# Padding the tiles of v to 128 rows, and moving weight-conversion passes and batch loads later

## The chip, the cores and the metric

The kernel runs on one core of a Trainium2 chip. The metric is the device time of one execution in microseconds (us). Engines are named as in the profile: PE (TensorE matmul), PEld (its weight loads), DVE (VectorE), ACT (ScalarE), POOL (GpSimd) and SP (SyncE, which issues nearly all DMAs here). L578 means line 578 of the kernel.

## The reference, cut to what matters

```python
# attention: 4 batches, 8 heads, 576 positions, head size 64
mask_plain = (rel >= 0) & (rel < 32)                       # heads 0..3
mask_dil   = (rel >= 0) & (rel < 128) & (rel % 4 == 0)     # heads 4..7
attn = softmax(where(mask, q @ k.T / 8, -1e9))
x = (attn @ v) laid out as (2304 tokens, 512)
x = ((x @ w_a) * (x @ w_b)) @ w_out                        # 512 -> 1536 -> 512
# top-1 of 8 experts by cosine similarity; gate = softmax probability of the chosen one
out[mask_e] = gate * (relu(x @ w1[e]) @ w2[e])             # 512 -> 1024 -> 512
```

The weights `w_a`, `w_b` and `w_out` come in as 64-bit floats, every other array as 32-bit floats.

## The kernel before, in words

**Attention in tiles of 64 queries.** The host reorders the dilated heads so that both masks become a band: a tile of 64 queries meets 96 keys. A batch has 9 tiles. q and k come in groups of three tiles (`qkt`, 128 rows, 832 KB), v in groups of three tiles (`vt`, 96 rows of keys by 3 tiles by 512 columns, 576 KB). A tile goes through scores (PE), row maxima (`amx`, DVE) and their scaled copy (`least`, POOL), `exp` (four activations on ACT), `norm` (two small DVE operations, then a POOL multiply, L559), `trans` (PE transposes into one PSUM bank `tp`, then an ACT copy to `aT`), `av` (PE, L474 or L578) and `oevac` (ACT and DVE write x0 as a high and a low part).

**Every large product is three matmuls.** A 32-bit operand is split into a high part (ACT, L660) and the remainder (DVE or POOL, L661); `mm3` (L702 to L704) multiplies high by high, high by low and low by high.

**Order of the work.** The schedule is manual: each engine runs its instructions in program order. Batch 0's attention stands by itself at the start (loop at L1185, up to about 33 us), with its loads, the load of the first weights and a few warm-up matmuls between. Then come, for each batch b, twelve steps `f_step(b, f)` (x @ w_a, x @ w_b for 128 of the 1536 columns, their product g) and `x1_run` (times `w_out`). In the steps of batch b the attention of batch b+1 runs beside, as five pairs of tiles (the last pair has one tile). For b = 0 a pair takes an odd and an even `f`: pair p opens in step 2p+1 (called here the opening step: maxima, exp(0), norm(0)) and goes on in step 2p+2 (the closing step: exp(1), norm(1), trans(0)); trans(1) and av come at the start of the next opening step. In the code's own words the opening step has `odd` = 0, since b = 0 counts with a lag of one.

**One step of batch 0 on PE.** `mm(0,0)`, then in an opening step av of the pair before and the scores of this one, `mm(1,0)`, in a closing step trans(0), then `mm(0,1)`, `mm(1,1)`. Each `mm` is 12 matmuls into one of four PSUM banks; ACT's `a_copy` and DVE's `g_evac` (L745) empty them, ACT makes gh (L748) and POOL makes gl (L749) from g.

**The conversion.** Step n of batch 0 also converts the 64-bit weights of step n+2 (`conv_steps`, L627): a scale pass on ACT (L640), then on DVE a shift pass (L642), a sign pass (L644) and a low-word pass (L646), each over 128x1024 words. The next step's `ab_split` splits what the step before converted, so its high half on ACT waits for the low-word pass. `conv(cg, k)` issues the next k of the four passes. A load of 1 MB (`conv_load`) and a store of the converted 512 KB (`conv_store`) go with each.

**Before the change** the passes stand: in a closing step the scale pass ahead of exp(1), the shift pass ahead of norm(1), the sign pass after norm(1), the low-word pass at the end; in an opening step the scale and shift passes ahead of `ab_split`, the sign pass after `oevac` (ahead of exp(0) in the program, though on another engine), the low-word pass at the end.

**Buffers.** The pool `ld` has two buffers each for `qkt` and `vt`; a third load waits for the tile that used the buffer. The pool `ab` has two tiles for the split weights.

Of the kernel before, what the change touches and what calls it, by code (L numbers as in the profile page):

```python
# [8 lines left out]
F32 = mybir.dt.float32  # L9
# [8 lines left out]
B, H, S, D = 4, 8, 576, 64  # L18
# [63 lines left out]
def fused_kernel(ctx: ExitStack, tc: tile.TileContext, qk, v, wab, wout, w1, w2, emb, tau, cst, msk, out, dbg=None):  # L82
# [279 lines left out]
    ap = ab_ctx.enter_context(tc.tile_pool(name="ab", bufs=2, side="right"))  # L362
# [10 lines left out]
    qkt, vt = {}, {}  # L373

    ld_seq = [(b, g) for b in range(B) for g in range(3)]
    ld_pos = [0, 0]
# [8 lines left out]
    def load_v():  # L385
        if ld_pos[1] < len(ld_seq):
            b, g = ld_seq[ld_pos[1]]
            ld_pos[1] += 1
            vt[b, g] = ld.tile([96, 3, 512], F32, tag="v", name="vt")
            nc.sync.dma_start(out=vt[b, g], in_=v[b, g])  # L390

    x0 = {}
# [4 lines left out]
    class Attn:  # L397
# [69 lines left out]
        def av(self):  # L467
            b, j = self.b, self.j
            t, jj = vt[b, j // 3], j % 3
            self.o = ps.tile([128, 4, 64], F32, tag="mm2" if self.early and j % 2 else "av", name="av")  # L470
            for pr in range(4):
                for p in range(2):
                    h = 2 * pr + p
                    nc.tensor.matmul(  # L474
                        out=self.o[64 * p:64 * p + 64, pr, :],
                        lhsT=t[:, jj, 64 * h:64 * h + 64],
                        rhs=self.aT[:, pr, 64 * (p ^ pr % 2):64 * (p ^ pr % 2) + 64],
                        start=True, stop=True,
                    )
# [14 lines left out]
    class AttnPair:  # L494
# [76 lines left out]
        def av(self):  # L571
            self.o = ps.tile([128, 4, 64 * self.n], F32, tag="av", name="av")
            for i, j in enumerate(self.js):
                t, jj = vt[self.b, j // 3], j % 3
                for pr in range(4):
                    for p in range(2):
                        h = 2 * pr + p
                        nc.tensor.matmul(  # L578
                            out=self.o[64 * p:64 * p + 64, pr, 64 * i:64 * i + 64],
                            lhsT=t[:, jj, 64 * h:64 * h + 64],  # L580
                            rhs=self.aT[i][:, pr, 64 * (p ^ pr % 2):64 * (p ^ pr % 2) + 64],
                            start=True, stop=True,
                        )
# [23 lines left out]
    def conv_load(i):  # L607
        if i < len(conv_src):
            if i < NF and i % 3 == 2:
                c64[i] = mp.tile([128, 2048], I32, tag="wo", name="c64w", bufs=1)  # L610
            elif i in (NF + 2, NF + 3):
                c64[i] = ap.tile([128, 2048], I32, tag="ab", name="c64a")
            else:
                c64[i] = cv.tile([128, 2048], I32, tag="c64", name="c64")
            nc.sync.dma_start(out=c64[i], in_=conv_src[i].bitcast(I32))
# [34 lines left out]
    def conv(gen, n=4):  # L650
        for _ in range(n):
            next(gen, None)

    def ab_load(n):
        if NF <= n < n_ab:
            ab_raw[n] = raw_tile("abr")
            nc.sync.dma_start(out=ab_raw[n], in_=wab32[n % NF])
# [65 lines left out]
    def f_step(b, f, pairs, extra, extra2):  # L723
        n = b * NF + f
        acc = acc_pre if n == 0 else {}
        lag = 1 if b == 0 else 0
        p, odd = divmod(f - lag, 2)
        cur = pairs[p] if 0 <= p < len(pairs) else None
        prv = pairs[p - 1] if not odd and 0 <= p - 1 < len(pairs) else None

        def mm(c, hf):
            for k in range(2 if (c, hf) in acc else 0, 4):
                ab_mm(n, acc, c, hf, k)

        kept = {}

        def a_copy(hf):
            kept[hf] = ap.tile([128, HALF], F32, tag="a", name="a")
            nc.scalar.activation(out=kept[hf], in_=acc[0, hf], func=AF.Copy)

        def g_evac(hf):
            g = ap.tile([128, HALF], F32, tag="g", name="g")
            c = hf * HALF + CARRY * (1 - b % 2)
            t = slice(c, c + HALF)
            nc.vector.tensor_tensor(out=g, in0=kept[hf], in1=acc[1, hf], op=ALU.mult)  # L745

            def low():
                nc.scalar.activation(out=g_hl[0][:, f, t], in_=g, func=AF.Copy)  # L748
                nc.gpsimd.tensor_tensor(out=g_hl[1][:, f, t], in0=g, in1=g_hl[0][:, f, t].bitcast(F32), op=ALU.subtract)  # L749

            g_low.append(low)

        if f - lag in (3, 6, 9):
            load_qk()
        if f - lag in (5, 8, 11):
            load_v()
        if f < NF - 2:
            ab_load(n + 2)
        if b == 0 and n < 10:
            conv_load(n + 4)  # L760
        if n == NF - 1:
            conv_load(NF + 2)
        if b == 0:
            conv_store()
        cg = iter(())
        if b == 0:
            cg = conv_steps(n + 2)
        if cur is not None and odd:
            conv(cg, 1)
            cur.exp(1)  # L770
            conv(cg, 1)
            cur.norm(1)
            conv(cg, 1)
        if prv is not None:
            prv.trans(1)
        if not odd or cur is None:
            conv(cg, 2)
        if n == 0:
            for q in range(4):
                ab_split_part(1, q)  # L780
        elif f < NF - 1:
            ab_split(n + 1)
        elif b == 0:
            wo_split(0)
        mm(0, 0)
        a_copy(0)
        if not odd:
            if cur is not None:
                cur.open()
            if prv is not None:  # L790
                prv.av()
            if cur is not None:
                cur.scores()
                cur.least_of()
            if prv is not None:
                prv.oevac()
            conv(cg, 1)
        g_lows()
        mm(1, 0)
        if cur is not None and not odd:  # L800
            cur.exp(0)
        g_evac(0)
        if cur is not None and odd:
            cur.trans(0)
        g_lows()
        for x in extra:
            x()
        mm(0, 1)
        a_copy(1)
        for x in extra2:  # L810
            x()
        mm(1, 1)
        if cur is not None and not odd:
            cur.norm(0)
        g_evac(1)
        del ab_hl[n]
        conv(cg)
# [347 lines left out]
    with tc.manual_schedule():  # L1165
# [17 lines left out]

        early_conv = conv_all()
        for i in range(NJ + LAG + 1):  # L1185
            if i in (3, 6, 9):
                load_qk()
            if i in (4, 6, 9):
                load_v()
            if i == CONV1:  # L1190
                conv_load(1)
                nc.sync.dma_start(out=c_sb, in_=cst)
            if i == 6:
                conv_load(2)
            if i < NJ:
                gr[i].scores(early=True)
            if 1 <= i < NJ + 1:
                gr[i - 1].exp()
            if LAG <= i < NJ + LAG:
                gr[i - LAG].trans()  # L1200
                gr[i - LAG].tevac()
            if LAG + 1 <= i:
                gr[i - LAG - 1].av()
            keep_warm(N_WARM if i < 4 else N_WARM_LATE if i < WARM_TO else 0, "mm1" if (i + 1 - LAG) % 2 else "tp")
            if 1 <= i < NJ + 1:
                gr[i - 1].norm()
            if i == NJ + LAG:
                conv(early_conv, CONV_STEPS[i])
            if LAG + 1 <= i:
                gr[i - LAG - 1].oevac()  # L1210
            if i < NJ + LAG:
                conv(early_conv, CONV_STEPS[i])
            for q in range(4):
                if SPLIT0[q] == i:
                    ab_split_part(0, q)
            if i in PRE:
                for k in range(2):
                    ab_mm(0, acc_pre, PRE.index(i), 0, k)
        for _ in early_conv:
            pass  # L1220
        load_v()

        router = None
# [197 lines left out]
def layout(inputs):  # L1421
# [13 lines left out]
    kT = np.zeros((B, 128, 4, S + 32), np.float32)  # L1435
    kT[..., 32:] = kp.reshape(B, 4, 2, S, D).transpose(0, 2, 4, 1, 3).reshape(B, 128, 4, S)
    qk = np.zeros((B, 3, 128, 4, 416), np.float32)
    vb = np.zeros((B, 3, 96, 3, 512), np.float32)
    vz = np.zeros((B, S + 32, 512), np.float32)
    vz[:, 32:] = vp.transpose(0, 2, 1, 3).reshape(B, S, 512)  # L1440
    for g in range(3):
        qk[:, g, :, :, :192] = qT[..., 192 * g:192 * g + 192]
        qk[:, g, :, :, 192:] = kT[..., 192 * g:192 * g + 224]
        for i in range(3):
            j = 3 * g + i
            vb[:, g, :, i] = vz[:, 64 * j:64 * j + 96]
    wab = np.stack([bits['moe_w_a'], bits['moe_w_b']], 0).reshape(2, 4, 128, NF, 128).transpose(3, 2, 1, 0, 4).reshape(NF, 128, 1024)
    wo = bits['moe_w_out'].reshape(NPAIR, 2, 128, DM).transpose(0, 2, 1, 3).reshape(NPAIR, 128, 1024)

# [54 lines left out]
```

## Time and profile before

| | |
|---|---|
| median of 3 runs | 792.83 us (792.18, 792.83, 796.73) |
| the profiled execution | 793.86 us, of which the span of the trace is 792.0 us |
| PE busy | 774.6 us, 98% |
| DVE, ACT, POOL busy | 518.8, 410.1, 206.2 us |
| granted TensorE clock, mean | 0.995 |
| moved by DMA | 136.18 MB, 172 GB/s over the span |

The profile has the busy time of each engine, slices of the span, the chain of work that ended last, and the trace behind it, which gives waits by pair of lines, the timeline of an engine, and busy times of any stretch. A busy time is a sum over the whole span; which engine sets the pace is read stage by stage.

### The profile page before, as it was taken

The page shows a single profiled execution, that of the slowest core. Times are in us where ns is not written, and L with a number is a line of the kernel's source. Part 1 is how long each engine was busy: PE and PEld are TensorE (multiplying, and loading weights), DVE is VectorE, ACT ScalarE, POOL GpSimd, SP SyncE. Part 2 cuts the span into 40 slices and gives each one's busy share as a digit, 9 for nine tenths or more (in the row PEclk, how much of TensorE's full clock was granted, in tenths as well). Part 3 has the DMA queues.
Part 4 walks back from the last instruction along what each step waited for, and adds up shares of the span by engine and source line. Part 5 has one row for each costly group of instructions (what it writes and reads, how often), then busy time and mean ns, then how long its engine had stood idle before and what let it go on. Part 6 is the DMA issues. An engine that isn't in the chain of part 4 may idle for free.

```text
span 792.0 us, 15979 instructions
## 1 busy us (share of the span) xinstructions
PE 774.6 (98%) x6122; PEld 723.5 (91%) x6122; DVE 518.8 (66%) x1155; ACT 410.1 (52%) x993; POOL 206.2 (26%) x251
## 2 busy tenths in 40 slices
PE   8989999999999999999999999999999999999995
PEld 4789998899999889999889999999898999999993
DVE  5788888758986228887627874455564566566570
ACT  5757774366653136665234443455463655665651
POOL 3454443023442204443222225331000001111110
PEclk9999999999999999999999999999999999999998
DMA  9987877497732323222152222635574554755720
GB/s 285 317 254 235 283 259 272 185 329 231 258 124 85 133 83 113 93 81 81 63 174 97 81 81 99 247 134 176 204 249 157 181 177 139 251 157 165 237 79 26
DMA packets 40294, 136.18 MB, mean 172 GB/s; under 512 B 4083, under 2 KB 4339, under 8 KB 37776
## 3 DMA queue, kind: packets, MB, share of 16 engines
q1 hardware_dynamic: 37120, 125.54, 48.4%
q0 software_dynamic: 3088, 9.52, 3.2%
q8 instruction: 50, 0.82, 0.4%
q14 instruction: 36, 0.29, 0.1%
HBM read 109.67 MB, written 25.80 MB: 171 GB/s over the span
## 4 chain that ended last, share of the span: by engine, by line
PE 84%; DMA 9%; issue 4%; DVE 1%; ACT 1%; POOL 0%; POOLq 0%; DVEq 0%; ACTq 0%
PE mm L702 13%; PE mm L703 12%; PE mm L704 12%; DMA out_dram<-yo,ixi 5%; PE xr L702 5%; PE xr L703 5%; PE xr L704 4%; PE hp L704 3%; PE hp L703 3%; PE hp L702 3%; PE av L578 2%; DMA c<-in_wab_dram 2%; PE ytp L703 2%; PE xm L704 2%; PE ytp L704 2%
## 5 line engine op out<-in xcount | busy, mean ns | idle before, releaser
L702 PE MATMUL mm<-x0h,ab 128*128 128x288 f32 x768 | 230.8, 301 | 1.0 <-DVE g L745 1.0
L704 PE MATMUL mm<-x0h,ab 128*128 128x288 f32 x768 | 226.5, 295 | 0.3 <-DVE ab L661 0.3
L703 PE MATMUL mm<-x0l,ab 128*128 128x288 f32 x768 | 226.2, 295 | 0.0
L702 PEld LDWEIGHTS mm<-x0h,ab 128*128 128x128 f32 x768 | 144.1, 188 | 3.5 <-DVE g L745 1.2
L704 PEld LDWEIGHTS mm<-x0h,ab 128*128 128x128 f32 x768 | 144.1, 188 | 0.9 <-DVE ab L661 0.5
L703 PEld LDWEIGHTS mm<-x0l,ab 128*128 128x128 f32 x768 | 144.2, 188 | 0.2
L749 POOL TENSOR_TENSOR gl<-g,gh 128x288 fp32r<-128x288 f32 x96 | 90.6, 946 | 131.6 <-ACT gh L748 128.6
L661 DVE TENSOR_TENSOR wl<-raw,wh 128x1024 fp32r<-128x1024 f32 x60 | 73.0, 1222 | 53.4 <-ACT wh L660 53.2
L661 DVE TENSOR_TENSOR wo<-wor,wo 128x512 fp32r<-128x512 f32 x60 | 47.0, 785 | 63.6 <-ACT wo L660 58.8
L660 ACT ACTIVATE wo<-wor 128x512 fp32r<-128x512 f32 x60 | 37.8, 631 | 86.0 <-PE xr L704 57.4
L1120 POOL DMA_INDIRECT out_dram<-yo,ixi x23 | 26.4, 1146 | 205.6 <-ACT yo L1119 160.3
L661 DVE TENSOR_TENSOR ab<-abr,ab 128x1024 fp32r<-128x1024 f32 x46 | 58.9, 1281 | 29.7 <-ACT ab L660 29.7
L745 DVE TENSOR_TENSOR g<-a,mm 128x288 f32<-128x288 f32 x96 | 43.2, 450 | 41.4 <-PE mm L704 17.0
L702 PE MATMUL hp<-xTh,wh 128*128 128x352 f32 (+6 forms) x224 | 68.9, 308 | 0.0
L748 ACT ACTIVATE gh<-g 128x288 fp32r<-128x288 f32 x96 | 42.9, 447 | 47.9 <-DVE g L745 47.4
L703 PE MATMUL hp<-xTl,wh 128*128 128x352 f32 (+6 forms) x224 | 67.7, 302 | 0.0
L704 PE MATMUL hp<-xTh,wl 128*128 128x352 f32 (+6 forms) x224 | 67.6, 302 | 0.0
L660 ACT ACTIVATE wh<-raw 128x1024 fp32r<-128x1024 f32 x64 | 67.1, 1054 | 0.0
L660 ACT ACTIVATE ab<-abr 128x1024 fp32r<-128x1024 f32 (+1 forms) x54 | 51.4, 961 | 23.2 <-PE mm L704 16.1
L702 PE MATMUL xr<-wo,gh 128*128 128x512 f32 x156 | 61.0, 391 | 0.0
L703 PE MATMUL xr<-wo,gh 128*128 128x512 f32 x156 | 60.9, 390 | 0.0
L704 PE MATMUL xr<-wo,gl 128*128 128x512 f32 x156 | 60.8, 390 | 0.0
(239 smaller groups left out, 1654.5 us busy)
## 6 DMA issues: line engine op xcount, KB each, us to landing
raw<-in_w_dram SPq DMA_DIRECT2D x64, 512.0 KB, 4.1
abr<-wab SPq DMA_DIRECT2D x36, 512.0 KB, 3.2
wor<-wout SPq DMA_DIRECT2D x24, 512.0 KB, 3.6
qkt<-in_qk_dram SPq DMA_DIRECT2D x12, 832.0 KB, 11.0
c<-in_wab_dram SPq DMA_DIRECT2D x8, 1024.0 KB, 11.4
vt<-in_v_dram SPq DMA_DIRECT2D x12, 576.0 KB
xs<-rows SPq DMA_DIRECT2D x8, 781.5 KB
wab<-abr SPq DMA_DIRECT2D x12, 512.0 KB, 6.4
```

Source lines behind the costliest of these rows:

```text
L578: nc.tensor.matmul(out=self.o[64 * p:64 * p + 64, pr, 64 * i:64 * i + 64], lhsT=t[:, jj, 64 * h:64 * h + 64], rhs=self.aT[i][:, pr, 64 * ( ...
L660: nc.scalar.activation(out=hi, in_=raw, func=AF.Copy)
L661: (eng or nc.vector).tensor_tensor(out=lo, in0=raw, in1=hi.bitcast(F32), op=ALU.subtract)
L702: nc.tensor.matmul(out=out_, lhsT=lh, rhs=rh, start=first, stop=False)
L703: nc.tensor.matmul(out=out_, lhsT=lh, rhs=rl, start=False, stop=False)
L704: nc.tensor.matmul(out=out_, lhsT=ll, rhs=rh, start=False, stop=last)
L745: nc.vector.tensor_tensor(out=g, in0=kept[hf], in1=acc[1, hf], op=ALU.mult)
L748: nc.scalar.activation(out=g_hl[0][:, f, t], in_=g, func=AF.Copy)
L749: nc.gpsimd.tensor_tensor(out=g_hl[1][:, f, t], in0=g, in1=g_hl[0][:, f, t].bitcast(F32), op=ALU.subtract)
L1120: nc.gpsimd.indirect_dma_start(out=out, out_offset=bass.IndirectOffsetOnAxis(ap=self.ixi[e][:m, t:t + 1], axis=0), in_=yo[:m, :], in_offse ...
```

## The change

The tiles of v are allocated and stored with 128 rows (the host fills rows 96 to 127 with zeros) and the matmuls read the first 96. The third v tile takes a tile of the `ab` pool. In the first stage both remaining v loads of batch 0 are issued at i = 4, the constants after the load of q and k at i = 6, and the loads of batch 1 that stood at i = 9 come after the loop; the last v load after the loop goes to step 2. In `f_step` the conversion passes are placed anew: in a closing step none ahead of exp(1) and norm(1), the scale and shift passes after `a_copy(0)`, the sign pass after `g_evac(0)`, the low-word pass at the end as before; in an opening step the scale and shift passes after exp(0) and `g_evac(0)`, the sign pass ahead of norm(0), the low-word pass at the end. Steps 0 and 11, which open or continue no pair, keep their order.

```diff
@@ load_v
-            vt[b, g] = ld.tile([96, 3, 512], F32, tag="v", name="vt")
+            if ld_pos[1] == 3:
+                vt[b, g] = ap.tile([128, 2048], F32, tag="ab", name="vt")[:, :1536].rearrange("p (j c) -> p j c", j=3)
+            else:
+                vt[b, g] = ld.tile([128, 3, 512], F32, tag="v", name="vt")
@@ Attn.av and AttnPair.av
-                        lhsT=t[:, jj, 64 * h:64 * h + 64],
+                        lhsT=t[:96, jj, 64 * h:64 * h + 64],
@@ f_step
         if f < NF - 2:
             ab_load(n + 2)
+        if n == 2:
+            load_v()
...
         if cur is not None and odd:
-            conv(cg, 1)
             cur.exp(1)
-            conv(cg, 1)
             cur.norm(1)
-            conv(cg, 1)
         if prv is not None:
             prv.trans(1)
-        if not odd or cur is None:
+        if cur is None:
             conv(cg, 2)
...
             if prv is not None:
                 prv.oevac()
-            conv(cg, 1)
+            if cur is None:
+                conv(cg, 1)
+        elif cur is not None:
+            conv(cg, 2)
         g_lows()
         mm(1, 0)
         if cur is not None and not odd:
             cur.exp(0)
         g_evac(0)
+        if cur is not None:
+            conv(cg, 1 if odd else 2)
         if cur is not None and odd:
             cur.trans(0)
...
         mm(1, 1)
         if cur is not None and not odd:
+            conv(cg, 1)
             cur.norm(0)
         g_evac(1)
@@ the first stage
-            if i in (3, 6, 9):
+            if i == 3:
                 load_qk()
-            if i in (4, 6, 9):
+            if i == 4:
+                load_v()
                 load_v()
             if i == CONV1:
                 conv_load(1)
+            if i == 6:
+                load_qk()
+                conv_load(2)
                 nc.sync.dma_start(out=c_sb, in_=cst)
-            if i == 6:
-                conv_load(2)
...
         for _ in early_conv:
             pass
+        load_qk()
         load_v()
@@ layout (host)
-    vb = np.zeros((B, 3, 96, 3, 512), np.float32)
+    vb = np.zeros((B, 3, 128, 3, 512), np.float32)
-            vb[:, g, :, i] = vz[:, 64 * j:64 * j + 96]
+            vb[:, g, :96, i] = vz[:, 64 * j:64 * j + 96]
```

## Rows read from the trace of the kernel before

**Rows 1.** The page's busy times by engine (share of the span, instructions).
```profile
PE 774.6 (98%) x6122; PEld 723.5 (91%) x6122; DVE 518.8 (66%) x1155; ACT 410.1 (52%) x993; POOL 206.2 (26%) x251
```
**Rows 2.** Busy us of each engine by stretch, then granted clock, DMA share, GB/s.
```profile
80.00:100.00 20.00, 20.00 (x204) 19.57 (x203) 16.85 (x29) 14.33 (x43) 8.77 (x11) 1.00 0.80 268
...
750.00:792.00 42.00, 32.17 (x224) 29.85 (x222) 18.46 (x61) 13.77 (x31) 6.32 (x6) 0.91 0.15 51
```
**Rows 3.** The three longest waits of PE: us in total, times, longest.
```profile
PE atp L567 <- POOL s L559: 1.3, 1, 1.3
...
PE av L474 <- DMA vt<-in_v_dram: 1.0, 1, 1.0
...
PE mm L702 <- DVE g L745: 1.0, 1, 1.0
```
**Rows 4.** Stretches of 1 us: a load of qkt, then one of vt.
```profile
6.00:7.00 1.00, 1.00 (x21) 0.55 (x20) 0.00 (x0) 0.00 (x0) 0.00 (x0) 1.00 1.01 416
...
16.00:17.00 1.00, 1.00 (x20) 0.78 (x19) 0.98 (x3) 1.00 (x6) 0.32 (x2) 1.00 1.12 211
```
**Rows 5.** Timeline of SP: start, us, line, what is issued.
```profile
19.73 0.33 SPq L390 DMA_DIRECT2D vt<-in_v_dram  x1
```
**Rows 6.** Timeline of DVE, then ACT, near 29 us: start, us, what [idle before].
```profile
27.72 1.51 DVE L646 SCALAR_TENSOR_TENSOR abr<-c,abr 128x1024 uint32<-128x1024 uint32 x1
...
29.80 0.73 ACT L660 ACTIVATE ab<-abr 128x256 fp32r<-128x256 f32 x2
```
**Rows 7.** Timeline of DVE, then ACT, near 44 us.
```profile
42.45 1.23 DVE L646 SCALAR_TENSOR_TENSOR abr<-c64w,abr 128x1024 uint32<-128x1024 uint32 x1
...
44.32 1.13 ACT L640 ACTIVATE c<-c 128x1024 f32<-128x1024 f32 x1 [4.17 <-DMA c<-in_wab_dram]
```
**Rows 8.** The chain of waits in order: start, us; trans(0) of pairs 0, 1, 2.
```profile
53.41 0.64 PE atp L567 x4
...
69.66 0.44 PE atp L567 x4
...
85.71 0.44 PE atp L567 x4
```
**Rows 9.** Timeline of ACT, opening step of pair 2 and the next step.
```profile
75.63 1.06 ACT L660 ACTIVATE ab<-abr 128x1024 fp32r<-128x1024 f32 x1 [0.17 <-DVE abr L646]
...
78.89 0.34 ACT L550 ACTIVATE s<-sc,least 128x96 f32<-128x96 f32 x1 [0.83 <-POOL least L544]
...
79.86 0.35 ACT L550 ACTIVATE s<-sc,least 128x96 f32<-128x96 f32 x1
...
82.29 1.15 ACT L640 ACTIVATE c64w<-c64w 128x1024 f32<-128x1024 f32 x1
...
85.91 0.39 ACT L739 ACTIVATE a<-mm 128x288 f32<-128x288 f32 x1
```
**Rows 10.** Timeline of DVE in the same opening step.
```profile
75.51 0.69 DVE L642 TENSOR_SCALAR abr<-c 128x1024 uint32<-128x1024 uint32 x1
...
79.84 1.42 DVE L644 SCALAR_TENSOR_TENSOR abr<-c,abr 128x1024 uint32<-128x1024 uint32 x1
...
81.73 0.18 DVE L558 RECIPROCAL asm<-asm 128x4 f32<-128x4 f32 x1
...
83.05 1.80 DVE L646 SCALAR_TENSOR_TENSOR abr<-c,abr 128x1024 uint32<-128x1024 uint32 x1
```
**Rows 11.** Timeline of POOL in the same opening step.
```profile
79.35 0.82 POOL L749 TENSOR_TENSOR gl<-g,gh 128x288 fp32r<-128x288 f32 x1
...
82.94 0.82 POOL L559 TENSOR_TENSOR s<-s,asm 128x384 f32<-128x384 f32 x1
```
**Rows 12.** Stretches of 1 us at the end, columns as in Rows 2.
```profile
782.00:783.00 1.00, 0.17 (x1) 0.00 (x0) 0.00 (x0) 0.69 (x1) 0.00 (x0) 1.00 0.00 0
...
784.00:785.00 1.00, 0.00 (x0) 0.00 (x0) 0.00 (x0) 0.00 (x0) 0.20 (x1) 0.67 0.25 90
785.00:786.00 1.00, 0.00 (x0) 0.00 (x0) 0.00 (x0) 0.00 (x0) 0.00 (x0) 0.50 0.24 94
```

More of the change, by code (lines that the diff above doesn't have):

```diff
@@ L579, in av @@
                             out=self.o[64 * p:64 * p + 64, pr, 64 * i:64 * i + 64],
-                            lhsT=t[:, jj, 64 * h:64 * h + 64],
+                            lhsT=t[:96, jj, 64 * h:64 * h + 64],
                             rhs=self.aT[i][:, pr, 64 * (p ^ pr % 2):64 * (p ^ pr % 2) + 64],
```

## The prediction, on record before the result

> **What bounds the kernel now.** I read the busy times first: PE is busy 98% of the span [rows 1]. By stages there are two exceptions. The last 10 us hold only the tail of the output [rows 2], which the change does not touch. The waits of PE name the other: transposes that wait for POOL's norm, an av that waits for a load of v, a matmul that waits for `g_evac`, 1.3, 1.0 and 1.0 us, each once [rows 3]. All three fall before 54 us, the last ahead of the trans(0) at 53.41 [rows 8]. From there to the tail PE hardly waits; in 80 to 100 us it is busy 20.00 of 20.00 us, but DVE is busy 16.85 beside it [rows 2]. So there is little to win (the three waits, 3.3 us), and a batch-0 stage in which DVE has about 3 us to spare in 20. The change reorders DVE's and ACT's work in exactly that stage.
>
> What paces that stage is seen from trans(0), which comes once per pair: pair 1 at 69.66, pair 2 at 85.71 us, so 16.05 us per pair, PE's own work [rows 8].
>
> **Part 1: 128 rows of v, and the early loads.** A load of q and k moves 416 GB/s, but a stretch in which v loads moves 211 [rows 4], with the DMA engines busy in both. The nearest row for a load of 128 full rows is that of q and k, so I take 786 KB at 416, 1.9 us, where 590 KB at 211 took 2.8; if padding does not change the rate it is 3.7. The third v load is issued at 19.73 us, when its buffer comes free [rows 5], and PE's av waits 1.0 us for it [rows 3]. After the change it is issued right behind the second load, near 11 us, into a tile that nothing used before, so it lands long before 27 us by either price. Late next: the first split of weights on ACT runs at 29.80, while its source is complete at 27.72 + 1.51 = 29.23 [rows 6]. So 0.57 us comes through, not 1.0. The tile that v borrows is written again by the split of step 1's weights, which stands behind all of batch 0's attention on each engine: no wait. The narrower matmul operand is the same 96 rows as before: nothing. Constants issued later are first used in `x1_run`: nothing. The loads moved past the loop, and the one moved to step 2, feed batch 1, whose first scores are in step 1 and whose first av is in step 3; on SP each takes 0.33 us to issue [rows 5], with no buffer to wait for, as its last readers are in batch 0. If that cover went, a load of 2 to 4 us would stand ahead of an av.
>
> **Part 2: the scale pass and the first opening step.** In step 1 ACT stands 4.17 us for a weight load, until 44.32 [rows 7], because the scale pass comes ahead of `ab_split` and of `a_copy(0)`. Moved behind exp(0), it holds up none of them; the load also lands earlier, as a load of q and k and one of v are no longer ahead of it. Then the split's high half can start when the last pass of the step before ends: 42.45 + 1.23 = 43.7 [rows 7], less the 0.57, so 43.1.
>
> From there I go along the new order, with T the end of the low-word pass, durations from the opening step of pair 2. High half, low half, maxima, `least`: exp(0) starts 78.89 - 75.63 = 3.3 after the high half starts, so T + 3.4. Exp lasts until 79.86 + 0.35, 1.3 us. Only now the scale pass, 1.15 [rows 9], and the shift pass, 0.69 [rows 10]. Meanwhile ACT makes gh, and POOL wants to make gl, 0.82 [rows 11].
>
> Here one fact of the trace decides. POOL's tensor work and DVE's passes over SBUF do not overlap: the sign pass at 79.84 lasted 1.42 us, and ends 1.1 us after POOL's gl (79.35 + 0.82 = 80.17); the low-word pass at 83.05 lasted 1.80 and ends 1.1 after POOL's norm (82.94 + 0.82) [rows 10, 11]. A pass alone takes 1.23 at most [rows 7]. So each POOL operation that becomes ready while DVE works goes ahead of DVE's next pass. Hence gl 0.8, the sign pass 1.2, norm's two small operations 0.35 (its second is 0.18 [rows 10]), POOL's norm 0.8: trans(0) can start at T + 3.4 + 1.3 + 1.15 + 0.7 + 0.8 + 1.2 + 0.35 + 0.8 = T + 9.7. I allow 0.05 us of overlap at each of seven handovers: T + 9.35. For T = 43.1 that is 52.4, where it was 53.41 [rows 8]: 1.0 us won in all, more than half of it part 1's. PE, whose work starts 0.57 earlier, then stands for 1.3 + 1.0 - 1.0 + 0.57 = 1.9 us, in one piece instead of two.
>
> **Part 3: the later pairs.** Before, the scale and shift passes ran in time that DVE and ACT otherwise spent waiting for each other: the shift pass at 75.51 lies beneath the high half at 75.63, which waits for the same low-word pass [rows 9, 10]. Moved, both stand in line. The low-word pass of the opening step ends at T + 9.7 + 1.2 = T + 10.9, and the next split waits for it. Closing step: high half 1.1, `a_copy` 0.4, scale pass 1.15 [rows 9], shift 0.7, gl 0.8, sign pass 1.2, the other gl 0.8, low-word pass 1.2: 7.35. A pair then takes 18.2 us, if each operation of POOL gets in the way; less the same allowance at fourteen handovers, 17.5. If none does, norm's 0.8 and three times gl's 0.8 go, but `g_evac` (an estimate: as long as ACT's copy of the same tile, 0.4 [rows 9]) stands in their place at three: 18.2 - 3.2 + 1.2 - 0.7 = 15.5. I take 17.5: the rows of this very step show the interference each time the two meet.
>
> PE has 16.05 us of work per pair, so a chain of 17.5 sets the pace, and trans(0) comes 1.45 us later with each pair. Five pairs make four intervals: 5.8 us. With 1.0 won before it, the change is 4.8 us to the worse at the last trans(0). After it the steps and `x1_run` have the same order as before, and PE is again the bound, so nothing is given back; what DVE is late by at the change of stage I leave in the range (up to 0.7). Batches 1 and 2 convert nothing.
>
> Sum against the profiled execution: 793.86 + 4.8 = 798.7. Its time is 1.03 above the median of the runs, so 797.6 against the median.
>
> **The rivals.**
> *PE stays the bound (not slower).* If POOL gets between the passes at less than two places of a pair, the pair takes 16.05 or less. The point that decides is a chain of 16.05. For it: the lower bound, 15.5. Against: the prolonged passes [rows 10]. Then only the 1.0 of the start remains: 791.8.
> *All three waits of PE go.* If the chain in step 1 is also shorter by those 1.9 us and PE stays the bound, 0.57 + 1.0 + 1.3 = 2.9 us are won: 789.9. For it: ACT's 4.17 us of standing is what the last two go back to. Against: norm(0) now stands behind a scale pass that stood ahead.
> *PE's clock falls.* At the end of the kernel PE finishes at 782.17; it is granted 1.00 in that slice, 0.67 in 784 to 785, and 0.50 from 785, the 1.2 GHz level [rows 12]. The 1.9 us ahead of the first trans(0) come near that. The step's 24 matmuls after it, of the 96 of a pair, take at most a quarter of 16.05, 4.0 us, and at half the clock 4.0 more. In my forecast the next trans(0) waits for DVE anyway and hides most of that; where PE is the bound it is paid: 791.8 + 4.0 = 795.8. The Trainium skill, TensorE: Matmul & The Clock Gate, Part 1: The HAM clock gate, says that an idle engine goes back to half its clock and gets the full one again only after some sustained work; by that, this rival would be the rule rather than the exception. The shorter waits of the kernel before, 1.0 and 1.3 us each, went without it in the profile.
> *Padding does not raise the rate.* Then v costs more and gains nothing. The third v load still starts 8 us earlier, so at most part 1's 0.57 us goes, and the loads behind it end up to 2.7 us later (three times 0.9), ahead of users that the forecast moves later: 798.2, inside the forecast.
>
> **How the numbers follow.** Chances: forecast 0.62 (with 0.10 of it the fourth rival's form), PE stays the bound 0.20, all waits go 0.10, the clock 0.05, a pair above 18.2 us 0.03. The forecast's own range: a pair of 17.0 to 18.0 us, four times 0.5 either way, and 0.7 above: 795.6 to 800.3. The range over the cases leaves out the 0.10 of 789.9 and a tail above: 790.8 to 800.5. A change under 1% (7.9 us) is about what cannot be told from none here. Faster by more would need more than all of PE's waits outside the tail: 0.02. Slower by more needs a pair above 18.2 us, my upper bound: 0.07. Within 1%: 0.91.
>
> **What would show it.** Right, if the windows of 60 to 120 us show PE idle by 1 to 2 us per pair, PE's waits list transposes on POOL's norm about four or five times, trans(0) comes every 17 to 18 us, the third v load no longer holds up av, and ACT no longer stands 4 us for a weight load. v's stretches should show about 400 GB/s. Wrong, if trans(0) still comes every 16.05 us and PE is busy throughout from 60 us on; then POOL's operations found gaps that I do not see.

## The result: 0.9% slower

| | before | after |
|---|---|---|
| median | 792.64 us (791.35 to 796.73, 9 runs) | 799.31 us (798.98 to 799.79, 9 runs) |
| ratio to before, 95% interval | | 1.0088 [1.0074, 1.0102] |
| the profiled execution | 793.86 us, span 792.0 | 799.31 us, span 797.5 |
| first matmul of `x1_run`, batch 0 | 127.97 us | 131.75 us |
| first matmul of batch 1 | 161.61 us | 166.70 us |

The forecast was 797.6 us, slower by less than 1%. In the page of the changed kernel the busy times have hardly moved against [rows 1], so nothing is to be learnt from them:

```profile
PE 777.0 (97%) x6122; PEld 724.5 (91%) x6122; DVE 520.6 (65%) x1155; ACT 409.6 (51%) x993; POOL 200.1 (25%) x251
```

The stretches of the changed kernel, with the columns of [rows 2], show where PE stands: batch 0, in which it was busy 20.00 of 20.00 us, and (last line) the change from its steps to `x1_run`.

```profile
60.00:80.00 20.00, 19.44 (x237) 18.64 (x234) 15.79 (x27) 13.12 (x38) 6.37 (x9) 1.00 0.67 225
80.00:100.00 20.00, 19.18 (x194) 18.33 (x194) 15.64 (x30) 13.69 (x43) 7.54 (x11) 1.00 0.81 285
100.00:120.00 20.00, 19.15 (x181) 18.31 (x179) 16.11 (x26) 11.68 (x35) 7.08 (x8) 1.00 0.71 251
120.00:140.00 20.00, 18.69 (x123) 15.76 (x123) 17.59 (x21) 11.16 (x21) 9.49 (x10) 1.00 0.72 255
```

PE is idle by 0.6 to 0.85 us in each of the first three; the forecast's sign, 1 to 2 us per pair, was larger. DVE is *less* busy there than before (15.64 against 16.85 in 80 to 100 us): it does not run out of time, it waits. The waits of PE, which answer to [rows 3], have new entries; the wait of av for the load of v and the one for `g_evac` are gone:

```profile
PE atp L570 <- POOL s L562: 4.0, 4, 2.9
PE atp L570 <- ACT aT L572: 1.8, 3, 0.6
...
PE xr L706 <- DVE wo L664: 0.4, 1, 0.4
```

The timeline of PE gives trans(0) of pairs 0 to 4, where [rows 8] had 53.41, 69.66 and 85.71 (the timeline of the kernel before has 53.41, 69.50, 85.55, 101.59 and 117.15):

```profile
51.69 0.64 PE L570 MATMUL atp<-ident,s 128*96 128x128 f32 x4 [2.86 <-POOL s L562]
...
69.30 0.60 PE L570 MATMUL atp<-ident,s 128*96 128x128 f32 x4
...
86.42 0.64 PE L570 MATMUL atp<-ident,s 128*96 128x128 f32 x4 [0.20 <-POOL s L562]
...
103.68 0.64 PE L570 MATMUL atp<-ident,s 128*96 128x128 f32 x4 [0.22 <-POOL s L562]
...
120.91 0.64 PE L570 MATMUL atp<-ident,s 128*96 128x128 f32 x4 [0.68 <-POOL s L562]
```

The first comes 1.7 us earlier than before. Then a pair takes 17.1 to 17.6 us instead of 16.05, and the fifth is 3.8 us late. (These rows do not show all that PE loses: trans(1), at the start of the next opening step, waits 0.56 to 0.63 us for aT, the second line of the waits above.)

What a pair is made of is read from DVE's and POOL's timelines, here from the opening step at 62 us to the end of the closing step. DVE of the changed kernel (of the small operations, those of norm(1) and of the closing step's `g_evac` are shown):

```profile
65.19 0.69 DVE L645 TENSOR_SCALAR abr<-c64w 128x1024 uint32<-128x1024 uint32 x1 [1.11 <-ACT c64w L643]
65.92 1.71 DVE L647 SCALAR_TENSOR_TENSOR abr<-c64w,abr 128x1024 uint32<-128x1024 uint32 x1
...
68.22 1.69 DVE L649 SCALAR_TENSOR_TENSOR abr<-c64w,abr 128x1024 uint32<-128x1024 uint32 x1
69.83 0.15 DVE L560 TENSOR_SCALAR asm<-asm 128x4 f32<-128x4 f32 x1
70.02 0.18 DVE L561 RECIPROCAL asm<-asm 128x4 f32<-128x4 f32 x1
71.38 1.23 DVE L664 TENSOR_TENSOR ab<-abr,ab 128x1024 fp32r<-128x1024 f32 x1 [1.18 <-ACT ab L663]
72.73 0.69 DVE L645 TENSOR_SCALAR abr<-c 128x1024 uint32<-128x1024 uint32 x1
73.35 0.45 DVE L748 TENSOR_TENSOR g<-a,mm 128x288 f32<-128x288 f32 x1
73.71 1.46 DVE L647 SCALAR_TENSOR_TENSOR abr<-c,abr 128x1024 uint32<-128x1024 uint32 x1
75.09 0.44 DVE L748 TENSOR_TENSOR g<-a,mm 128x288 f32<-128x288 f32 x1
75.45 1.46 DVE L649 SCALAR_TENSOR_TENSOR abr<-c,abr 128x1024 uint32<-128x1024 uint32 x1
```

POOL beside it:

```profile
65.56 0.99 POOL L752 TENSOR_TENSOR gl<-g,gh 128x288 fp32r<-128x288 f32 x1 [1.56 <-ACT gh L751]
68.00 0.83 POOL L562 TENSOR_TENSOR s<-s,asm 128x384 f32<-128x384 f32 x1 [1.45 <-DVE asm L561]
...
73.10 0.98 POOL L752 TENSOR_TENSOR gl<-g,gh 128x288 fp32r<-128x288 f32 x1 [1.93 <-ACT gh L751]
74.34 1.49 POOL L752 TENSOR_TENSOR gl<-g,gh 128x288 fp32r<-128x288 f32 x1 [0.26 <-ACT gh L751]
```

Two things stand out. The shift pass waits 1.11 us for a scale pass that now stands behind exp(0) on ACT. And no sign or low-word pass takes the 1.23 us of a pass alone [rows 7]: each meets an operation of POOL. Low-word passes end at 42.17, 59.44, 76.91, 94.16 and 111.41 us, so the chain takes 17.3 us a round.

### The profile page after: what moved, and what is told of

It reads as the page before. It is cut to its first block, busy times and chain, and to the rows that moved or that the text cites. A ratio compares the mean times of both kernels' runs of the same rounds, so it can differ in the third digit from the quotient of the medians.

```text
span 797.5 us, 15980 instructions
## 1 busy us (share of the span) xinstructions
PE 777.0 (97%) x6122; PEld 724.5 (91%) x6122; DVE 520.6 (65%) x1155; ACT 409.6 (51%) x993; POOL 200.1 (25%) x251
## 3 DMA queue, kind: packets, MB, share of 16 engines
q0 software_dynamic: 3088, 9.52, 3.1%
## 4 chain that ended last, share of the span: by engine, by line
PE 76%; DMA 3%; issue 2%; DVE 1%; ACT 0%; POOLq 0%; POOL 0%; DVEq 0%
PE mm L705 10%; PE mm L706 10%; PE mm L707 10%; PE xr L706 4%; PE xr L705 4%; PE xr L707 4%; PE hp L706 3%; PE hp L707 3%; PE hp L705 3%; DMA out_dram<-yo,ixi 3%; PE ytp L706 2%; PE ytp L707 2%; PE ytp L705 2%; PE xm L707 2%; PE xm L705 2%
## 5 line engine op out<-in xcount | busy, mean ns | idle before, releaser
L664 DVE TENSOR_TENSOR ab<-abr,ab 128x1024 fp32r<-128x1024 f32 x46 | 56.4, 1227 | 38.6 <-ACT ab L663 38.5
```

What stands on the lines that cost most here:

```text
L664: (eng or nc.vector).tensor_tensor(out=lo, in0=raw, in1=hi.bitcast(F32), op=ALU.subtract)
```

## The experiments

Theory A is the forecast's: in batch 0 the round of passes over ACT, DVE and POOL sets the pair, and the opening step's new order made it longer than PE's 16.05 us. The kernel before was run again beside them: 792.1 us (23 runs) beside loads_only, order_only, opening_back and closing_back, 791.76 (21 runs) beside scale_first, no_gl, rows96 and warm, 792.23 (13 runs) beside gl_twice and scale_no_gl. Each ratio is to the runs beside it.

**The loads alone (loads_only).** The old order of passes in the changed kernel:

```
         if cur is not None and odd:
+            conv(cg, 1)
             cur.exp(1)
+            conv(cg, 1)
             cur.norm(1)
...
-        if cur is None:
+        if not odd or cur is None:
             conv(cg, 2)
...
```

> The change without its new order of the conversion passes (128 rows of v, v in the borrowed tile and the new order of loads stay). Theory A, the loss is the chain of DVE and ACT in the opening steps: the pairs take PE's 16.05 us again, the 1.5 us won before step 1 stay, and with the weight load landing before ACT's scale pass asks for it, PE's waits in steps 1 and 2 go as well: 3 to 4.5 us faster than the kernel before, 788 to 789.5. Rival B, the closing steps: the same here. Rival C, the wider v loads and their new places cost the time (more bytes, other transfers delayed): 797 or more.

Measured: 791.51 us (790.71 to 791.77), ratio 0.9989 [0.9978, 1.0]. A pair takes 16.05 us again (trans(0) at 51.10, 67.18, 83.23, 99.27, 114.83), so the loss is not in the loads. But the gain fell short of the 3 to 4.5 us expected. One reason is the base: I had counted from the profiled execution of before, which with more runs turns out 1.8 us above the median. The other is the first norm: POOL's `s` ends at 51.04 there, and PE still waits 1.3 us for it.

**The order alone (order_only).** The kernel before with the new order of passes and nothing else of the change.

> The kernel before with only the new order of the conversion passes (v with 96 rows, loads as before). A: the pairs take 17.3 us as in the changed kernel, and the 1.5 us that the loads win ahead of step 1 are missing: 799.5 to 801. B: the same. C: 792, no change.

Measured: 799.6 us (798.54 to 803.31), ratio 1.0107 [1.0085, 1.0129]; trans(0) at 52.40, 69.65, 86.88, 104.13, 121.36: 17.24 us a pair. The whole loss is the order's. PE stood 2.93 us ahead of the first trans(0) here, and its granted clock stayed at 1.00 behind that, so the pairs are as long without a fall of the clock:

```profile
54.00:56.00 2.00, 2.00 (x17) 2.00 (x16) 1.26 (x2) 2.00 (x4) 0.72 (x1) 1.00 0.69 102
```

**Which step's order (opening_back, closing_back).** The changed kernel with the old order in the opening steps, then in the closing steps alone:

```
 opening_back
-        if cur is None:
+        if not odd or cur is None:
             conv(cg, 2)
...
-            if cur is None:
-                conv(cg, 1)
+            conv(cg, 1)
...
-        if cur is not None:
-            conv(cg, 1 if odd else 2)
+        if cur is not None and odd:
+            conv(cg, 1)
...
         if cur is not None and not odd:
-            conv(cg, 1)
             cur.norm(0)
```

> The changed kernel with the passes of the opening steps (maxima, exp(0), norm(0)) where they were before; the closing steps keep the new order. A: the opening step's chain from low-word pass to low-word pass falls from 10.6 to about 9 us, the closing one stays at 6.9, a pair is at or below PE's 16.05: within 1.5 us of the run with all passes back, 788 to 791. B, the closing steps' order makes the loss: 797 to 799.

> The changed kernel with the passes of the closing steps (exp(1), norm(1), trans(0)) where they were before; the opening steps keep the new order. A: the closing chain gets 0.3 to 0.5 us shorter, the opening one stays at 10.5: a pair of about 17.0 us, 797 to 799. B: 788 to 791.

Measured: opening_back 791.03 us (790.48 to 791.89), ratio 0.9991 [0.9982, 1.0], trans(0) at 50.20, 66.29, 82.34, 98.39, 113.94 (the time lies at the upper edge of the range given); closing_back 798.17 (797.82 to 798.5), ratio 1.0079 [1.0063, 1.0095], a pair near 17.1. The opening step's order costs it; the closing step's new order costs nothing while there is room, and some 0.1 us a pair where there is none (17.1 against 17.25).

**One link of it (scale_first).** In the opening step only the scale pass goes back ahead of the split:

```
         if cur is None:
             conv(cg, 2)
+        elif not odd:
+            conv(cg, 1)
...
-            conv(cg, 1 if odd else 2)
+            conv(cg, 1)
```

> The changed kernel, but in the opening steps the scale pass alone goes back ahead of ab_split; shift, sign and low-word pass stay at their new places. Theory A (the loop that sets the pair is the chain of passes, and the link that makes it too long is the scale pass standing behind exp(0) on ACT): the shift pass no longer waits 1.11 us for the scale pass (the row of the changed kernel at 65.19), so a pair takes 17.25 - 1.1 = 16.15 or TensorE's own 16.05, trans(0) of pair 4 begins at 116 to 117 instead of 120.9, and the time is 792 to 794.5. Theory B (the places of the three DVE passes behind the urgent work cost it, wherever the scale pass stands): the pair stays at 17.0 or more and the time at 797.5 to 799.5.

Measured: 793.49 us (792.72 to 794.48), ratio 1.002 [1.001, 1.0029]; trans(0) of pair 4 at 115.76. DVE of this kernel, at the place of the 65.19 above:

```profile
62.49 0.44 DVE L748 TENSOR_TENSOR g<-a,mm 128x288 f32<-128x288 f32 x1
62.85 0.68 DVE L645 TENSOR_SCALAR abr<-c64w 128x1024 uint32<-128x1024 uint32 x1
63.56 1.81 DVE L647 SCALAR_TENSOR_TENSOR abr<-c64w,abr 128x1024 uint32<-128x1024 uint32 x1
```

The shift pass follows `g_evac` without the 1.11 us, and low-word passes (58.29, 74.66, 90.89, 107.09 at the end of closing steps) come every 16.2 to 16.4 us. Theory A, to the size of that one wait.

**The other link (no_gl, gl_twice).** In batch 0, POOL's gl left out, or made twice:

```
 no_gl
-                nc.gpsimd.tensor_tensor(out=g_hl[1][:, f, t], ...)
+                if b:
+                    nc.gpsimd.tensor_tensor(out=g_hl[1][:, f, t], ...)
...
+            if b == 0 and i == 0:
+                nc.gpsimd.memset(g_hl[1].bitcast(F32), 0.0)
...
 gl_twice
-                nc.gpsimd.tensor_tensor(out=g_hl[1][:, f, t], ...)
+                for _ in range(2 if b == 0 else 1):
+                    nc.gpsimd.tensor_tensor(out=g_hl[1][:, f, t], ...)
```

> The changed kernel without POOL's gl in batch 0 (x1_run of batch 0 multiplies with gh twice instead, so that TensorE does the same number of matmuls; gl is set to zero once at the start of x1_run). Theory B2 (POOL's and DVE's operations hold each other up, as 1.69 and 1.71 us for passes that take 1.46 elsewhere suggest, and that is what lengthens the pair): the pair falls from 17.25 to 16.05 to 16.5 and the time to 791.5 to 796. Theory A (the order of the passes on DVE and ACT does it; gl only stretches two of them by 0.25 us): the pair falls by 0.5 us at most, to 16.75 to 17.2, and the time is 797 to 799.3.

> The changed kernel, but POOL makes gl of batch 0 twice each time (four operations of 0.81 us more in a pair). Theory A (a POOL operation that runs beside a DVE pass lengthens the pass by the time that they lie together, less 0.14 us, and the passes are the chain that sets the pair): the pair rises from 17.3 to 18.0 to 19.0, trans(0) of pair 4 begins at 124 to 128, and the time is 802 to 806. Rival (leaving gl out helped for another reason, such as TensorE's or ACT's load, and POOL has time to spare): the pair stays at 17.1 to 17.5 and the time at 799 to 800.

Measured: no_gl 796.09 us (795.75 to 796.79), ratio 1.0052 [1.0037, 1.0067]; closing steps' low-word passes end at 42.04, 58.40, 74.97, 91.27 and 107.58, so a pair fell to 16.3 to 16.6. That is theory B2's pair, and a miss for my bound of 0.5 us. The time lies 0.1 us above that theory's range. The edit's own zeroing of gl has a part in it: beside this operation (first row, POOL) a shift pass (second row, DVE) took 3.37 us instead of 0.69, and PE stood 1.3 us, until 124.01, for the `g_evac` behind it.

```profile
116.52 6.53 POOL L867 MEMSET gl<- 128x7680 f32 x1
...
120.23 3.37 DVE L645 TENSOR_SCALAR wor<-c 128x1024 uint32<-128x1024 uint32 x1
```

DVE of no_gl, in the opening step (65.92 above) and in the closing step (73.71 and 75.45 above):

```profile
64.88 1.23 DVE L647 SCALAR_TENSOR_TENSOR abr<-c64w,abr 128x1024 uint32<-128x1024 uint32 x1
...
72.25 1.22 DVE L647 SCALAR_TENSOR_TENSOR abr<-c,abr 128x1024 uint32<-128x1024 uint32 x1
...
73.75 1.22 DVE L649 SCALAR_TENSOR_TENSOR abr<-c,abr 128x1024 uint32<-128x1024 uint32 x1
```

Three passes shorter by 0.24, 0.24 and, in the opening step, 0.48 us: 0.96 a pair, which is the difference. I had counted only the stretch of 1.69 and 1.71 over 1.46, though 1.46 was itself stretched.

gl_twice took 807.76 us (807.42 to 808.24), ratio 1.0178 [1.0137, 1.0219]; low-word passes end at 43.78, 62.40, 81.20, 99.78 and 118.38, 18.6 to 18.8 us a pair, as expected. The time is 1.8 us above the range given (the last trans(0), at 128.44, 0.4 us), because the chain ahead of the first pair (43.78 against 42.17) and `x1_run`'s waits (1.4 us against 0.4) grew as well.

**Both links (scale_no_gl).**

> Both edits in one: the scale pass of the opening steps ahead of ab_split again, and no gl in batch 0 (x1_run of batch 0 multiplies with gh twice, gl is set to zero at its start). Each alone took the pair from 17.3 to 16.2 and 16.4 us. Theory A (both are links of one chain, which TensorE's 16.05 us cut off from below): the chain falls to 15.3 or so, a pair takes TensorE's 16.05, its waits for aT go, trans(0) of pair 4 begins at 114.3 to 115.2, and the time is 791 to 792.5. Rival (something else holds the pair at 16.2 to 16.4, and each of the two only reached that): trans(0) of pair 4 at 115.5 to 117, the time 793 to 796.

Measured: 790.63 us (789.92 to 791.01), ratio 0.9969 [0.9951, 0.9987]; trans(0) at 49.15, 65.93, 81.98, 98.03 and 113.58: 16.05 us a pair between 65.93 and 98.03. The time is 0.4 us and the last trans(0) 0.7 us below the range given; the first pair is earlier than in any other kernel here. So the two links add up, until PE's own work bounds the pair. (This ratio is not one of a usable kernel: gl is missing.)

**The rows of v (rows96).** loads_only with v in tiles of 96 rows:

```
-                vt[b, g] = ld.tile([128, 3, 512], F32, tag="v", name="vt")
+                vt[b, g] = ld.tile([96, 3, 512], F32, tag="v", name="vt")
...
```

> The changed kernel with the old order of passes (its time 791.5) and with v in tiles of 96 rows again; the new places of the loads stay. If the 128 rows are what makes a load of v short (1.9 us instead of 2.8): the stretch from 10 to 20 us falls back from 404 GB/s to about 320, the first scores begin 0.3 to 0.9 us later, trans(0) of pair 0 as much later, and the time is 791.9 to 793. If the new places of the loads are what gains: 791.0 to 791.8, the start as with 128 rows.

Measured: 791.18 us (790.57 to 791.62), ratio 0.9991 [0.9982, 1.0], against 0.9989 [0.9978, 1.0] with 128 rows: no difference. Two stretches of loads_only, with the columns of [rows 2]:

```profile
10.00:20.00 10.00, 9.40 (x158) 6.28 (x160) 7.81 (x26) 8.22 (x46) 5.01 (x9) 1.00 0.97 389
...
16.00:17.00 1.00, 1.00 (x26) 0.70 (x17) 0.95 (x5) 1.00 (x4) 0.48 (x1) 1.00 1.00 406
```

The same two of rows96:

```profile
10.00:20.00 10.00, 9.49 (x158) 6.19 (x160) 7.82 (x26) 8.33 (x45) 5.02 (x9) 1.00 1.01 308
...
16.00:17.00 1.00, 1.00 (x22) 0.70 (x23) 0.95 (x4) 1.00 (x4) 0.64 (x1) 1.00 0.98 240
```

The rate does rise with 128 rows, from 308 to 389 GB/s in the ten microseconds and from 240 to 406 in the one, and nobody waits for it: trans(0) of pair 0 at 51.24 and 51.10, and neither kernel has PE's wait for v. So the 128 rows gain nothing that can be measured; whatever the loads gain comes from their places.

**The clock (warm).** Twelve idle matmuls just ahead of trans(0) of pair 0.

> The changed kernel with 12 idle matmuls of 128 x 512 just ahead of trans(0) of pair 0, where TensorE stands for 2.87 us at 48.8. They should keep the granted clock at 1.00 in the stretch 53 to 57 us, in which it fell to 0.50. Theory A (the chain of passes sets the pairs, so TensorE's slow stretch of some 3 us is made up while it would wait anyhow): 798.8 to 799.6, trans(0) of pair 4 at 120.5 to 121.2. Rival C (the fall of the clock is part of the loss): TensorE gains back what it lost there, 1 to 2 us, the time is 797 to 798.3, and trans(0) of pair 4 begins at 119 to 120.

Measured: 799.56 us (799.32 to 799.7), ratio 1.0098 [1.0082, 1.0113]. The stretches behind PE's standing in the changed kernel, the granted clock third from the end:

```profile
53.00:54.00 1.00, 1.00 (x6) 1.00 (x6) 0.10 (x2) 1.00 (x2) 0.83 (x1) 0.53 0.56 66
54.00:56.00 2.00, 2.00 (x10) 2.00 (x9) 1.87 (x3) 2.00 (x4) 0.37 (x1) 0.50 0.70 209
```

and in this one:

```profile
53.00:54.00 1.00, 1.00 (x10) 1.00 (x9) 0.30 (x3) 0.86 (x1) 0.52 (x1) 1.00 0.00 0
54.00:56.00 2.00, 1.86 (x14) 1.62 (x13) 1.64 (x2) 2.00 (x5) 0.36 (x2) 1.00 0.78 197
```

The idle matmuls keep the clock at 1.00, and the time does not move. PE's fall to half its rate was real: counted from the end of the last pass of step 0 (42.17 in the changed kernel, 42.50 here), the next trans(0) came 0.4 us later with it (69.30 against 69.20, 27.13 against 26.70 us after that end). One pair further nothing of it is left (86.42 and 86.73, 44.25 and 44.23 us after), since there trans(0) waits for the chain in both.

## Why the prediction was right

**Part 3, the pair (right, its size in part by luck).** 17.5 us was forecast, 17.3 measured, 5.8 us over four intervals against 69.22 - 63.74 = 5.5. The interference of POOL and DVE that I read from [rows 10, 11] is what no_gl and gl_twice move, and the scale pass behind exp(0) is the other half. Without both the chain would lie under PE's 16.05 us; either alone brings it to 16.2 to 16.6. The sum of 18.2 was closer than the reasons for it, and "do not overlap" was too strong: gl does not add its whole 0.8 us each time, as I wrote. A pass is lengthened by the time that it lies beside the POOL operation, less about 0.14 us: the sign pass at 65.92 lies beside gl until 66.55, 0.63 us, and is 0.49 longer than 1.22; the low-word pass at 68.22 lies beside `s` until 68.83, 0.61, and is 0.47 longer; the sign pass at 73.71 lies beside gl until 74.08, 0.37, and is 0.24 longer. And where DVE was first, POOL waits: the gl at 74.34 took 1.49 us instead of 0.81, until 0.66 us after that sign pass ended (73.71 + 1.46 = 75.17). The Trainium skill, SBUF — State Buffer, SBUF: two separate sides, says that a DVE operation with two SBUF inputs and a GpSimd operation that reads SBUF exclude each other: the one that starts first has the ports that they share for its whole instruction, and the other is blocked. These rows agree, except for the 0.14 us, whose cause no run here shows. The three gl of the sum, 0.8 us each, thus cost 0.96 us a pair here and not 2.4. What the sum had too much there, it lacked elsewhere: in the closing step, where it had 1.6 us for two gl, the rows have 0.48 us of lengthening, two `g_evac` of 0.45 us on DVE, and norm(1)'s small operations (to 70.20), behind which the split's high half began at 70.28, 0.37 us after the low-word pass. The closing step took the 7.0 us forecast (7.35 less the allowance) by terms that happened to cancel.

**Part 2, the first pair (right in number, not in its reason).** T is again the end of step 0's low-word pass. ACT no longer stands 4.17 us for a load [rows 7]. Its rows in step 1 of the changed kernel:

```profile
42.28 1.06 ACT L663 ACTIVATE ab<-abr 128x1024 fp32r<-128x1024 f32 x1 [3.64 <-DVE abr L649]
...
46.83 1.14 ACT L643 ACTIVATE c<-c 128x1024 f32<-128x1024 f32 x1
```

From T = 42.17 trans(0) came at T + 9.52, forecast T + 9.35, and T + 9.73 before. But the new order is not what won there. In loads_only, with the old order, the load has landed when the scale pass asks for it, ahead of the split:

```profile
39.28 1.14 ACT L643 ACTIVATE c<-c 128x1024 f32<-128x1024 f32 x1
...
43.03 1.06 ACT L663 ACTIVATE ab<-abr 128x1024 fp32r<-128x1024 f32 x1 [2.61 <-DVE abr L649]
```

Its trans(0) came at T + 8.19 (51.10 - 42.91), as in rows96 (51.24 - 43.05). So the earlier load alone ends ACT's standing, and the new order costs 1.3 us in the first opening step as well; with the old loads it wins 0.14 (order_only, 52.40 - 42.81 = 9.59). PE stood 2.86 us ahead of the first trans(0) instead of 1.9. The rival of the falling clock came about in this execution, in the form that the forecast named: 0.50 from 54 us on, but the chain hid it. After the 2.93 us of order_only it did not.

**Part 1 (not shown).** T was 1.5 us earlier than before, forecast 0.57, but these executions cannot tell this from none. Up to T the new order changes nothing, so order_only runs the same program there as the kernel before; its T was 42.81, against 43.68. The kernels loads_only and opening_back, which are alike up to T as well, had 42.91 and 42.03. Executions of one and the same start thus lie 0.9 us apart. Nor does av wait for v in order_only, though the load is issued as late (19.85 us): the 1.0 us of [rows 3], from which part 1 went out, comes in one execution with these loads and not in another. (The one that has it was 1.8 us above the median.) And my reason, the shorter load of v by its 128 rows, falls with rows96.

**The change of stage (mis-sized).** Up to 0.7 us was allowed; it was 1.3: `x1_run` of batch 0 took 34.95 us instead of 33.64. The last conversions of wout are DVE's too, and come late; PE's list above has 0.4 us of waiting for them, and how the rest divides I have not traced. The second split's low half begins 1.8 us after `x1_run`'s first matmul in the kernel before:

```profile
129.78 1.30 DVE L661 TENSOR_TENSOR wo<-wor,wo 128x512 fp32r<-128x512 f32 x1
```

and 3.3 us after it in the changed one:

```profile
135.08 0.69 DVE L664 TENSOR_TENSOR wo<-wor,wo 128x512 fp32r<-128x512 f32 x1
```

In sum -1.7 + 5.5 + 1.3 = 5.1 us at batch 1's first matmul, forecast 4.8; the span grew by 5.5, and the last 0.4 I have not traced. Against loads_only, which has the same loads, the order's cost adds up without the loads' part: 1.3 in the first opening step, 5.5 in the pairs and 1.3 here, less the 0.7 by which T came earlier, are 7.4 us at batch 1's first matmul (166.70 against 159.29). Against the medians the loss is 6.7 us, as the execution of before that I counted from was a long one: the sum of terms was closer than the base.

No usable version beat the kernel before by more than can be measured: loads_only, rows96 and opening_back lie 0.1% below it, each interval ending at 1.0.

## What to carry to other kernels

An operation moved "behind the urgent ones" leaves the slack that it ran in: before moving a pass, follow the round of dependences of one loop turn over all engines and compare its length with the busiest engine's work. Here the scale and shift passes of the opening step had been free because they lay beneath a wait of ACT for the same data. When DVE has slack in the busy shares and yet PE waits, look at POOL's timeline beside the lengthened DVE operations, and price the overlap and not POOL's whole operation.

## What the runs showed that I had not expected

- Executions with the old places of the loads spread widely: 790.6 to 796.75 us for the kernel before (7 of 66 above 794), 798.54 to 803.31 for order_only. With the new places, in any order and with 96 or 128 rows, each kernel's spread was 0.4 to 1.8 us (790.57 to 791.62 for rows96, 798.98 to 799.79 after). So the new places take away the long executions; which of the loads does it wasn't tried.
- In the stretch from 16 to 17 us the DMA engines were as busy with 96 rows of v as with 128 (0.98 and 1.00), at 240 against 406 GB/s, although a tile has only a quarter fewer rows.
- In the changed kernel PE's granted clock fell to half only once it worked again: 1.00 through the 2.86 us of standing (48.8 to 51.7) and until 53 us, 0.53 in 53 to 54. After a standing of nearly the same length closing_back (2.87 us) had the fall too, order_only (2.93 us) did not.
